# Convolution weights turned after the first k^T v, v loaded by ScalarE's queue, q of batch 1 turned by TensorE

## The chip, the cores and the metric

The kernel runs on one core of a Trainium2 chip. The metric is the device time of one execution in microseconds (us); before the change it is 333.07 us, the median of three runs (332.60 to 333.87). The profile shows one execution, with a span of 331.5 us.

## What is computed

Two blocks follow each other, on 8 batches, 8 heads, 576 tokens and a head width of 64; the 8 heads side by side are the 512 channels of the second block. The inputs q, k and v are float32; the weights of the second block come as float64.

```python
kv   = einsum('bhsd,bhse->bhde', k, v)               # 64 x 64 for each batch and head
out  = einsum('bhsd,bhde->bhse', q, kv)
x    = out / sqrt(mean(out * out, -1) + 1e-6) * g_norm
x    = x.transpose(0, 2, 1, 3).reshape(8, 576, 512)
gate = sigmoid(sum(conv_w[t] * x_shifted_by(4 - t) for t in range(5)))   # causal, by channel
y    = (gate * (x @ w_val)) @ w_out
```

## The kernel before, in words

All work is written as named steps, and the string PLAN at the head of the file lists them, with their arguments, in the order in which they are issued. No scheduler changes it at build time: each engine executes its own instructions in the order of the list, and waits for semaphores where a step needs what another engine makes. The list itself was made by a planner outside the file. So a change of PLAN changes what each engine has queued behind what.

A batch goes through these steps. load_half, load_tails and load_q (or load_q_rows) bring k, v, their last 64 tokens, and q. kv_product (L433) forms k^T v for pairs of heads in the PSUM bank "kv", kv_copy (L453, on ScalarE) moves it into a block-diagonal matrix. q has to lie with its channels across the partitions: turn_q (L463) does this by VectorE's transposes of 32x32 blocks; for batch 0, turn_q_rows (L477) does it by TensorE, five groups of matmuls with the identity into "mm" banks, which sort_q (L487, ScalarE) copies into qT. raw_product (L494) multiplies qT by the matrix, 128 tokens at a time (chunks 0 to 3, and 4 with the last 64 tokens); square (ScalarE), sums (VectorE), powers (GpSimd) and normalise (VectorE for batch 0, ScalarE for the others) make x of it. turn_x and keep_x, or turn_blocks and move_blocks from batch 2 on, put x with its channels across the partitions; halo adds the tokens before. gate_start, four gate_tap and gate_end make the gate; val_product, or from batch 2 on val_fast with fewer multiplications, makes the values; gated multiplies; out_product, or fast_product for the last two batches, is the output projection, and store writes it.

PSUM has eight banks for four kinds (L226): one "kv", two "raw", one "tp", four "mm". The "mm" banks go round among turn_q_rows, val_product, out_product and, for batch 0, raw_product of the chunks 4, 1 and 0.

Before the first batch can be finished, the float64 weights must be made float32. stage_weight loads one piece, narrow_weight turns it in eight small steps 0 to 7: steps 1, 2 and 3 on ScalarE, the others on VectorE. For the convolution weights ("cw", 20 rows) there follow turn_cw (L410), one transpose on TensorE, and keep_cw (L415) on VectorE. They are first used by gate_start.

keep_warm n (L426) issues n matmuls of the identity with itself into the spare half of the "kv" bank. They compute nothing; they fill time in which TensorE would be idle. In the profile every float32 matmul has two records, so keep_warm 5 reads as "x10".

Loads are issued by three queues: SyncE's (SPq) for nearly all, ScalarE's (ACTq) for the first half of k and of v of batch 0 and for the first piece of the value weights, GpSimd's for the convolution weights and g_norm. load_q (L310) brings one pair of heads in four transfers of 32 partitions; load_q_rows (L324) brings four heads in one transfer of 128 partitions, with rows of 18 tokens. Both write into the three slots of the tile qs.

Of the kernel before, what the change touches and what calls it, by code (L numbers as in the profile page):

```python
# [20 lines left out]
stage_weight wval 0; warm_up; load_half k 0 1; load_half v 0 1; stage_weight wval 1; narrow_weight cw 0 0;  # L21
load_half k 1 0; narrow_weight cw 0 1; narrow_weight cw 0 2; load_half v 1 0; narrow_weight cw 0 3;
load_tails 1; narrow_weight cw 0 4; narrow_weight cw 0 5; narrow_weight cw 0 6; narrow_weight cw 0 7;
keep_warm 26; turn_cw; load_half k 1 1; load_half v 1 1; load_q 1 0; keep_warm 5; turn_q_rows 0 0;
turn_q_rows 0 1; sort_q 0 0; turn_q_rows 0 2; sort_q 0 1; kv_product 0 0; narrow_weight wval 0 0; keep_cw;
turn_q_rows 0 3; narrow_weight wval 0 1; sort_q 0 2; turn_q_rows 0 4; narrow_weight wval 0 2; load_q 1 1;
sort_q 0 3; keep_warm 4; kv_product 0 1; sort_q 0 4; load_q 1 2; kv_copy 0; narrow_weight wval 1 0;
narrow_weight wval 0 3; keep_warm 4; raw_product 0 3; narrow_weight wval 1 1; raw_product 0 2; square 0 3;
stage_weight wval 2; stage_weight wval 3; raw_product 0 4; sums 0 3; square 0 2; raw_product 0 1; square 0 4;
powers 0 3; sums 0 2; narrow_weight wval 1 2; narrow_weight wval 0 4; raw_product 0 0; square 0 1; sums 0 4;  # L30
narrow_weight wval 0 5; powers 0 2; square 0 0; normalise 0 3; narrow_weight wval 1 3; sums 0 1; keep_warm 5;
turn_x 0 3; powers 0 4; keep_x 0 3; normalise 0 2; sums 0 0; powers 0 1; keep_warm 5; turn_x 0 2;
normalise 0 4; narrow_weight wval 1 4; keep_x 0 2; narrow_weight wval 0 6; keep_warm 4; turn_x 0 4; powers 0 0;
kv_product 1 0; normalise 0 1; keep_x 0 4; turn_q 1 0; turn_x 0 1; narrow_weight wval 1 5; halo 0; load_q 1 3;
narrow_weight wval 0 7; kv_product 1 1; keep_x 0 1; normalise 0 0; turn_q 1 1; turn_x 0 0; val_product 0 0 1;
narrow_weight wval 1 6; stage_weight wout 0; keep_x 0 0; narrow_weight wval 1 7; gate_start 0 1; turn_q 1 2;
gate_start 0 2; val_product 0 1 1; load_q 2 1; narrow_weight wval 2 0; gate_tap 0 2 3; narrow_weight wval 2 1;
gate_tap 0 1 3; narrow_weight wval 2 2; val_product 0 0 0; gate_tap 0 1 2; gate_start 0 0; load_q 2 0;
gate_tap 0 2 2; narrow_weight wval 2 3; kv_copy 1; narrow_weight wval 3 0; turn_q 1 3; narrow_weight wval 3 1;
load_half k 2 0; narrow_weight wval 2 4; keep_val 0 0 1; keep_warm 6; raw_product 1 3; narrow_weight wval 3 2;  # L40
load_half v 2 0; narrow_weight wval 2 5; load_tails 2; raw_product 1 2; narrow_weight wval 2 6; square 1 3;
keep_val 0 1 1; val_product 0 1 0; sums 1 3; keep_val 0 0 0; narrow_weight wval 3 3; narrow_weight wval 2 7;
load_half v 2 1; powers 1 3; square 1 2; load_half k 2 1; narrow_weight wout 0 0; gate_tap 0 2 1; load_q 2 2;
val_product 0 2 1; sums 1 2; normalise 1 3; narrow_weight wval 3 4; powers 1 2; narrow_weight wval 3 5;
gate_tap 0 2 0; stage_weight wout 2; narrow_weight wout 0 1; keep_warm 3; raw_product 1 1;
narrow_weight wval 3 6; gate_tap 0 0 3; turn_x 1 3; square 1 1; val_product 0 2 0; narrow_weight wout 0 2;
sums 1 1; keep_x 1 3; narrow_weight wval 3 7; powers 1 1; normalise 1 2; gate_tap 0 1 1; val_product 0 3 1;
turn_q 2 0; gate_tap 0 1 0; normalise 1 1; load_q 2 3; raw_product 1 0; turn_q 2 1; turn_x 1 2; val_sums 0;
square 1 0; tail_and_kv 1; narrow_weight wout 0 3; stage_weight wout 1; sums 1 0; keep_x 1 2;
narrow_weight wout 0 4; powers 1 0; keep_val 0 1 0; gate_tap 0 0 2; keep_val 0 2 0; gate_end 0 1; val_sums 1;  # L50
keep_val 0 2 1; turn_x 1 1; turn_q 2 2; square 1 4; normalise 1 0; val_product 0 3 0; sums 1 4; load_q 3 1;
narrow_weight wout 2 0; powers 1 4; narrow_weight wout 0 5; gate_tap 0 0 1; keep_x 1 1; turn_q 2 3; kv_copy 2;
keep_warm 2; turn_x 1 0; load_q 3 0; normalise 1 4; val_sums 2; raw_product 2 3; narrow_weight wout 0 6;
keep_x 1 0; gate_tap 0 0 0; keep_val 0 3 1; turn_x 1 4; square 2 3; raw_product 2 2; narrow_weight wout 0 7;
load_half k 3 1; keep_x 1 4; narrow_weight wout 2 1; sums 2 3; load_half v 3 0; val_product 1 0 1;
gate_end 0 0; load_tails 3; powers 2 3; square 2 2; gated 0 0; narrow_weight wout 2 2; val_product 1 0 0;
gated 0 1; keep_val 0 3 0; load_half v 3 1; narrow_weight wout 2 3; load_half k 3 0; sums 2 2; gate_start 0 3;
stage_weight wout 3; narrow_weight wout 2 4; powers 2 2; normalise 2 3; val_product 1 1 1; load_q 3 2;
gate_tap 0 3 3; narrow_weight wout 1 0; narrow_weight wout 2 5; halo 1; keep_val 1 0 1; gate_tap 0 3 2;
keep_val 1 0 0; raw_product 2 1; normalise 2 2; turn_q 3 0; val_product 1 1 0; turn_q 3 1; load_q 3 3;  # L60
square 2 1; turn_blocks 2 3; narrow_weight wout 1 1; sums 2 1; val_product 1 2 1; keep_val 1 1 1;
gate_tap 0 3 1; narrow_weight wout 1 2; powers 2 1; keep_val 1 1 0; narrow_weight wout 2 6;
narrow_weight wout 1 3; turn_blocks 2 2; raw_product 2 0; gate_end 0 2; narrow_weight wout 1 4; normalise 2 1;
val_product 1 2 0; narrow_weight wout 2 7; narrow_weight wout 1 5; gated 0 2; square 2 0; gate_tap 0 3 0;
tail_and_kv 2; turn_blocks 2 1; gate_end 0 3; narrow_weight wout 3 0; keep_val 1 2 1; sums 2 0;
narrow_weight wout 3 1; narrow_weight wout 1 6; powers 2 0; narrow_weight wout 3 2; gated 0 3;
val_product 1 3 1; load_half k 4 0; narrow_weight wout 3 3; turn_q 3 2; load_half v 4 0; square 2 4; kv_copy 3;
load_half k 4 1; sums 2 4; narrow_weight wout 3 4; normalise 2 0; load_q 4 0; val_product 1 3 0; powers 2 4;
narrow_weight wout 3 5; turn_q 3 3; normalise 2 4; narrow_weight wout 3 6; raw_product 3 3; load_q 4 1;
narrow_weight wout 1 7; gate_start 1 0; turn_x 2 4; narrow_weight wout 3 7; raw_product 3 2; gate_start 1 1;  # L70
turn_blocks 2 0; keep_x 2 4; out_product 0 3; gate_tap 1 0 3; keep_val 1 2 0; move_blocks 2 3; load_tails 4;
keep_val 1 3 1; square 3 3; gate_tap 1 1 3; gate_start 1 2; sums 3 3; square 3 2; load_half v 4 1;
gate_tap 1 0 2; keep_val 1 3 0; powers 3 3; gate_tap 1 2 3; out_product 0 1; sums 3 2; gate_tap 1 1 2;
powers 3 2; normalise 3 3; gate_tap 1 0 1; gate_tap 1 2 2; gate_tap 1 0 0; keep_out 0 3; raw_product 3 1;
move_blocks 2 2; gate_tap 1 1 1; store 0 3; gate_end 1 0; out_product 0 0; gate_tap 1 2 1; square 3 1;
keep_out 0 1; gated 1 0; load_q 4 2; sums 3 1; gate_start 1 3; gate_tap 1 1 0; powers 3 1; gate_tap 1 3 3;
gate_end 1 1; out_product 0 2; turn_blocks 3 3; store 0 1; normalise 3 2; halo 2; gate_tap 1 3 2;
gate_tap 1 2 0; normalise 3 1; move_blocks 2 1; gate_tap 1 3 1; gated 1 1; raw_product 3 0; gate_end 1 2;
gate_tap 1 3 0; tail_and_kv 3; turn_q 4 0; gate_end 1 3; gated 1 2; keep_out 0 0; load_q 4 3; square 3 0;
gated 1 3; sums 3 0; out_product 0 5; weight_sums 0; kv_copy 4; powers 3 0; load_half v 5 1; turn_blocks 3 2;  # L80
square 3 4; store 0 0; sums 3 4; turn_blocks 3 1; powers 3 4; turn_q 4 1; normalise 3 0; move_blocks 2 0;
turn_q 4 2; out_product 0 4; keep_out 0 5; normalise 3 4; store 0 5; turn_q 4 3; keep_out 0 2; weight_sums 1;
turn_blocks 3 0; load_tails 5; turn_x 3 4; val_sums 3; raw_product 4 3; keep_x 3 4; move_blocks 3 3;
raw_product 4 2; square 4 3; load_q 5 0; out_product 0 6; sums 4 3; square 4 2; keep_out 0 4; sums 4 2;
gate_start 2 0; powers 4 3; x_sums 2 0; load_half k 5 0; gate_start 2 3; load_half k 5 1; x_sums 2 1;
gate_start 2 2; gate_tap 2 0 3; val_fast 2 0 0; gate_tap 2 2 3; val_fast 2 0 1; x_sums 2 3; val_keep 2 0 0;
# [100 lines left out]
def kernel(  # L187
# [11 lines left out]
    nc = tc.nc  # L199
# [7 lines left out]
    TB = 32  # L207
# [8 lines left out]
    TURNED_X = 2  # L216
# [608 lines left out]
```

## Time and profile before

| | us |
|---|---|
| time, median of three runs | 333.07 |
| span of the profiled execution | 331.5 |
| TensorE busy (96%) | 319.7 |
| VectorE busy (75%) | 247.0 |
| ScalarE busy (57%) | 189.6 |
| GpSimd busy (43%) | 142.8 |
| keep_warm, 64 matmuls in all | 20.5 |
| turning q of batch 0 on TensorE, 36 matmuls | 6.1 |
| the five copies of it on ScalarE | 2.6 |
| turning q of batch 1 on VectorE, 4 transposes | 3.1 |

The page of a profile gives busy time by engine, then the span in 40 slices with a digit for the busy tenths of each, then the chain of work that ended last. The chain is followed back from the last instruction: at each step to what released it, or to the instruction before it on its engine. A wait for several things is put down to the one that came last. Matmuls are pipelined, so that a busy TensorE isn't always at its peak; the row PEclk and the column of the clock tell at what share of full speed it was allowed to run.

### The profile page before, as it was taken

The numbers are of one execution on the slowest core, as the hardware profiler recorded it, in microseconds if no ns is written. First come the engines' busy times: TensorE is split into PE (matmuls) and PEld (weight loads), VectorE is DVE, ScalarE is ACT, GpSimd is POOL, SyncE is SP. The second block draws the span as 40 slices with busy tenths as digits, with TensorE's granted clock in tenths as the row PEclk, the third lists the DMA queues.
The fourth block names the chain that finished last, engine by engine and source line by source line (L and its number), as shares of the span: only waits on it lengthen the run. The fifth ranks groups of instructions, "written<-read, shape, count | busy, mean of one in ns | idle before, by whom it ended". The sixth has DMA issues, their size and how long they took to land.

```text
span 331.5 us, 6118 instructions
## 1 busy us (share of the span) xinstructions
PE 319.7 (96%) x2041; PEld 230.0 (69%) x2041; DVE 247.0 (75%) x434; ACT 189.6 (57%) x530; POOL 142.8 (43%) x185
## 2 busy tenths in 40 slices
PE   8498999999999999999999999999999999999994
PEld 8498988878854658756884767586544765868652
DVE  1203998999999969998989888978996179835711
ACT  1145487999879664676757655766652344142311
POOL 5002805536469869533985453854749200000000
PEclk9879999999999999999999999999999999999999
DMA  8997289989798778965799884325125203021323
GB/s 275 315 307 216 89 252 308 238 244 289 201 274 237 204 207 232 287 148 147 232 275 261 226 193 128 86 48 127 35 61 156 70 15 75 9 64 32 97 63 95
DMA packets 44127, 56.47 MB, mean 170 GB/s; under 512 B 15158, under 2 KB 33590, under 8 KB 44096
## 3 DMA queue, kind: packets, MB, share of 16 engines
q1 hardware_dynamic: 39120, 47.93, 52.3%
q0 software_dynamic: 3168, 6.32, 7.5%
q10 hardware_dynamic: 1808, 1.84, 1.8%
q8 instruction: 16, 0.26, 0.4%
q14 instruction: 15, 0.12, 0.1%
HBM read 40.33 MB, written 9.44 MB: 150 GB/s over the span
## 4 chain that ended last, share of the span: by engine, by line
PE 90%; POOL 2%; ACT 2%; DMA 2%; DVE 1%; issue 1%; POOLq 0%; ACTq 0%; DVEq 0%
PE out L686 25%; PE va L655 14%; PE raw L501 10%; PE val L605 8%; PE vc L655 7%; PE kv L441 5%; PE out L693 4%; PE a L750 4%; PE vb L655 4%; PE cb L750 3%; PE kv L430 3%; DMA w_cw<-in_moe_conv_w_dram 2%; PE qTps L483 2%; PE xTps L555 1%; POOL rt L529 1%; ACT x L540 1%
## 5 line engine op out<-in xcount | busy, mean ns | idle before, releaser
L529 POOL TENSOR_TENSOR rt<-ss,mhalf 128x8 f32<-128x8 f32 (+1 forms) x40 | 69.6, 1743 | 101.1 <-DVE ss L523 101.0
L593 DVE SCALAR_TENSOR_TENSOR gate<-xT,cwT,gate 128x576 f32<-128x576 f32 x128 | 100.5, 811 | 7.1 <-ACT gate L587 6.6
L686 PE MATMUL out<-wout,gv 128*128 128x512 f32 x192 | 85.6, 594 | 0.0
L686 PEld LDWEIGHTS out<-wout,gv 128*128 128x128 f32 x192 | 35.8, 190 | 39.7 <-issue 37.5
L540 ACT ACTIVATE x<-raw,rt 128x64 f32<-128x64 f32 x252 | 55.3, 345 | 6.9 <-POOL rt L529 6.6
L576 POOL DMA_DIRECT2D xT<-y x96 | 53.3, 561 | 12.0 <-issue 3.4
L523 DVE TENSOR_REDUCE ss<-sq 128x8 f32<-128x520 f32 (+1 forms) x40 | 25.2, 632 | 22.3 <-ACT sq L515 22.1
L501 PEld LDWEIGHTS raw<-kvbd,qT 128*128 128x128 f32 (+1 forms) x320 | 35.1, 180 | 7.9 <-issue 3.7
L501 PE MATMUL raw<-kvbd,qT 128*128 128x128 f32 (+1 forms) x320 | 38.1, 278 | 0.0
L605 PE MATMUL val<-xT,wval 128*128 128x288 f32 x128 | 32.6, 408 | 0.0
L515 ACT ACTIVATE sq<-raw 128x512 f32<-128x512 f32 (+1 forms) x40 | 22.7, 571 | 12.0 <-PE raw L501 11.9
L600 ACT ACTIVATE gate<-gate 128x576 f32<-128x576 f32 x32 | 22.5, 712 | 10.3 <-DVE gate L593 10.3
L701 ACT COPY ot<-out 128x512 f32<-128x512 f32 x28 | 16.4, 591 | 20.4 <-PE out L686 12.4
L605 PEld LDWEIGHTS val<-xT,wval 128*128 128x128 f32 x128 | 23.6, 190 | 6.1 <-DVE wval L387 0.2
L655 PE MATMUL va<-xs,vsum 128*128 128x288 f32 x96 | 27.2, 406 | 0.0
L618 DVE TENSOR_TENSOR gv<-gv,gate 128x576 f32<-128x576 f32 x32 | 23.7, 751 | 2.3 <-ACT gv L676 1.8
L587 ACT ACTIVATE gate<-xT,cwT 128x576 f32<-128x576 f32 x32 | 24.6, 790 | 1.2 <-DVE gv L618 0.8
L430 PE MATMUL kv<-ident 128*128 128x128 f32 x128 | 20.5, 323 | 2.8 <-ACT kvbd L456 1.4
L430 PEld LDWEIGHTS kv<-ident 128*128 128x128 f32 x128 | 19.0, 233 | 4.1 <-ACT kvbd L456 2.4
L655 PEld LDWEIGHTS va<-xs,vsum 128*128 128x128 f32 x96 | 18.1, 190 | 5.2 <-issue 0.5
L469 DVE STREAM_TRANSPOSE qT<-qs 128x512 f32<-128x512 f32 x24 | 16.7, 696 | 0.4 <-DMA qs<-in_q_dram 0.4
L583 POOL COPY xT<-xT 128x124 f32<-128x124 f32 x32 | 16.1, 541 | 1.7 <-DMA xT<-y 1.7
(114 smaller groups left out, 439.3 us busy)
## 6 DMA issues: line engine op xcount, KB each, us to landing
qs<-in_q_dram SPq DMA_DIRECT2D x112, 140.0 KB, 4.2
out_dram<-ot SPq DMA_DIRECT2D x140, 64.0 KB, 1.7
k<-in_k_dram SPq DMA_DIRECT2D x12, 512.0 KB, 5.8
v<-in_v_dram SPq DMA_DIRECT2D x12, 512.0 KB, 5.5
xT<-y POOLq DMA_DIRECT2D x96, 64.0 KB, 3.1
w_wout<-in_moe_w_out_dram SPq DMA_DIRECT2D x4, 512.0 KB, 7.8
y<-in_moe_w_val_dram SPq DMA_DIRECT2D x3, 512.0 KB, 4.6
qs<-in_q_dram SPq DMA_DIRECT2D x2, 576.0 KB, 4.8
```

What stands on the lines that cost most here:

```text
L430: nc.tensor.matmul(st["spare"].rearrange("p h d -> p (h d)")[:, 0:P], ident[:], ident[:], start=True, stop=True)
L501: nc.tensor.matmul(raw[row * m:(row + 1) * m, col * P:(col + 1) * P], st["qT", b][:, hp, c * P:c * P + m], kv_bd[b % 2][:, hp, :], start=T ...
L523: nc.vector.reduce_sum(out=ss[:, 0:n], in_=st["sq", b, c][:, 0:n], axis=AX.X)
L529: nc.gpsimd.tensor_tensor(out=rt[:, 0:n], in0=st["ss", b, c][:, 0:n], in1=mhalf[:, 0:n], op=ALU.pow)
L540: nc.scalar.activation(out=x[:, to * D:(to + 1) * D], in_=st["raw", b, c][:, h * D:(h + 1) * D], func=AF.Copy, scale=st["rt", b, c][:, h:h ...
L576: nc.gpsimd.dma_start(out=xTs[b % 2][i * TB:(i + 1) * TB, :, first:first + P], in_=y[a * TB:(a + 1) * TB, i])
L587: nc.scalar.activation(out=gate[:], in_=xTs[b % 2][:, jt, HALO:SX], func=AF.Copy, scale=cwT[:, K - 1, jt:jt + 1])
L593: nc.vector.scalar_tensor_tensor(out=gate[:], in0=xTs[b % 2][:, jt, tap * TB:tap * TB + S], scalar=cwT[:, tap, jt:jt + 1], in1=gate[:], op ...
L605: nc.tensor.matmul(val[:], wval[:, kc, jt * P:(jt + 1) * P], xTs[b % 2][:, kc, HALO + n * SV:HALO + (n + 1) * SV], start=(kc == 0), stop=( ...
L618: nc.vector.tensor_tensor(out=both, in0=both, in1=st["gate", b, jt][:], op=ALU.mult)
L655: nc.tensor.matmul(st[bank, "val", b, mj][:], weights_[:, k], tokens()[:, k], start=(n in (0, 1, 3) and k == 0), stop=(k == NK // 2 - 1), ...
L686: nc.tensor.matmul(po[:], gv[:, jt, first:first + P], wout[:, jt, :], start=(jt == 0), stop=(jt == NK - 1),)
```

## The change

It has four parts. The narrowing of the convolution weights, turn_cw and keep_cw move in PLAN behind the start of k^T v of batch 0; they stood in front of the turning of q. The second half of v of batch 0 is loaded by ScalarE's queue instead of SyncE's, and the first piece of the value weights by SyncE's instead of ScalarE's. q of batch 1 is loaded by load_q_rows and turned by turn_q_rows and sort_q, as that of batch 0 is, so that turn_q's form for it goes. And the rest of PLAN is planned anew around this: the same steps in another order. The number of fillers goes from 64 to 32. The purpose is that TensorE begins useful work with q as soon as q is there, and that VectorE is relieved of four transposes.

The plan is cut to its beginning, as far as the first product with the value weights; after it only the order changes.

```diff
 load_half k 0 0; stage_weight cw 0; load_q_rows 0 0; load_half v 0 0; load_q_rows 0 1; load_tails 0;
-stage_weight wval 0; warm_up; load_half k 0 1; load_half v 0 1; stage_weight wval 1; narrow_weight cw 0 0;
-load_half k 1 0; narrow_weight cw 0 1; narrow_weight cw 0 2; load_half v 1 0; narrow_weight cw 0 3;
-load_tails 1; narrow_weight cw 0 4; narrow_weight cw 0 5; narrow_weight cw 0 6; narrow_weight cw 0 7;
-keep_warm 26; turn_cw; load_half k 1 1; load_half v 1 1; load_q 1 0; keep_warm 5; turn_q_rows 0 0;
-turn_q_rows 0 1; sort_q 0 0; turn_q_rows 0 2; sort_q 0 1; kv_product 0 0; narrow_weight wval 0 0; keep_cw;
-turn_q_rows 0 3; narrow_weight wval 0 1; sort_q 0 2; turn_q_rows 0 4; narrow_weight wval 0 2; load_q 1 1;
-sort_q 0 3; keep_warm 4; kv_product 0 1; sort_q 0 4; load_q 1 2; kv_copy 0; narrow_weight wval 1 0;
-narrow_weight wval 0 3; keep_warm 4; raw_product 0 3; narrow_weight wval 1 1; raw_product 0 2; square 0 3;
-stage_weight wval 2; stage_weight wval 3; raw_product 0 4; sums 0 3; square 0 2; raw_product 0 1; square 0 4;
-powers 0 3; sums 0 2; narrow_weight wval 1 2; narrow_weight wval 0 4; raw_product 0 0; square 0 1; sums 0 4;
-narrow_weight wval 0 5; powers 0 2; square 0 0; normalise 0 3; narrow_weight wval 1 3; sums 0 1; keep_warm 5;
-turn_x 0 3; powers 0 4; keep_x 0 3; normalise 0 2; sums 0 0; powers 0 1; keep_warm 5; turn_x 0 2;
-normalise 0 4; narrow_weight wval 1 4; keep_x 0 2; narrow_weight wval 0 6; keep_warm 4; turn_x 0 4; powers 0 0;
-kv_product 1 0; normalise 0 1; keep_x 0 4; turn_q 1 0; turn_x 0 1; narrow_weight wval 1 5; halo 0; load_q 1 3;
-narrow_weight wval 0 7; kv_product 1 1; keep_x 0 1; normalise 0 0; turn_q 1 1; turn_x 0 0; val_product 0 0 1;
+load_half v 0 1; warm_up; keep_warm 16; turn_q_rows 0 0; load_half k 0 1; turn_q_rows 0 1; sort_q 0 0;
+turn_q_rows 0 2; stage_weight wval 0; sort_q 0 1; stage_weight wval 1; turn_q_rows 0 3; sort_q 0 2;
+turn_q_rows 0 4; load_q_rows 1 0; keep_warm 1; kv_product 0 0; load_q_rows 1 1; load_half k 1 0;
+narrow_weight cw 0 0; narrow_weight cw 0 1; load_half v 1 0; narrow_weight cw 0 2; load_tails 1;
+narrow_weight cw 0 3; sort_q 0 3; narrow_weight cw 0 4; keep_warm 5; kv_product 0 1; narrow_weight cw 0 5;
+sort_q 0 4; narrow_weight cw 0 6; narrow_weight cw 0 7; turn_cw; kv_copy 0; narrow_weight wval 0 0;
+narrow_weight wval 0 1; load_half k 1 1; keep_warm 3; raw_product 0 3; load_half v 1 1; narrow_weight wval 1 0;
+raw_product 0 2; keep_cw; stage_weight wval 2; square 0 3; stage_weight wval 3; narrow_weight wval 0 2;
+raw_product 0 4; sums 0 3; stage_weight wout 0; square 0 2; raw_product 0 1; powers 0 3;
+narrow_weight wval 1 1; sums 0 2; square 0 4; narrow_weight wval 0 3; keep_warm 2; turn_q_rows 1 0; square 0 1;
+powers 0 2; normalise 0 3; narrow_weight wval 1 2; sums 0 4; sort_q 1 0; keep_warm 2; turn_x 0 3; sums 0 1;
+turn_q_rows 1 1; powers 0 4; keep_x 0 3; normalise 0 2; narrow_weight wval 1 3; powers 0 1; turn_x 0 2;
+normalise 0 4; narrow_weight wval 0 4; turn_q_rows 1 2; keep_x 0 2; narrow_weight wval 1 4; turn_x 0 4;
+normalise 0 1; keep_x 0 4; narrow_weight wval 1 5; sort_q 1 1; keep_warm 3; raw_product 0 0; halo 0;
+narrow_weight wval 1 6; turn_x 0 1; narrow_weight wval 1 7; square 0 0; turn_q_rows 1 3;
+narrow_weight wval 0 5; sort_q 1 2; sums 0 0; keep_x 0 1; turn_q_rows 1 4; narrow_weight wval 0 6; powers 0 0;
+sort_q 1 3; kv_product 1 0; load_q 2 0; narrow_weight wval 0 7; sort_q 1 4; narrow_weight wval 2 0;
+kv_product 1 1; narrow_weight wval 2 1; normalise 0 0; narrow_weight wval 2 2; narrow_weight wval 3 0;
+val_product 0 0 1;
...
@@ load_half
-                (nc.sync if i else nc.scalar).dma_start(
+                (nc.sync if i and name == "k" else nc.scalar).dma_start(
@@ stage
-        (nc.gpsimd if key[0] == "cw" else nc.scalar if key == ("wval", 0) else nc.sync).dma_start(
+        (nc.gpsimd if key[0] == "cw" else nc.sync).dma_start(
@@ turn_q
-        if b < TURNED_X:
-            nc.vector.transpose(out=qT, in_=q[:, :, 0:TB])
-            return
```

## The prediction

> **What bounds the kernel now.** I read the page first: of a span of 331.5 us TensorE is busy for 319.7.
>
> ```profile
> PE 319.7 (96%) x2041; PEld 230.0 (69%) x2041; DVE 247.0 (75%) x434; ACT 189.6 (57%) x530; POOL 142.8 (43%) x185
> PE   8498999999999999999999999999999999999994
> PEclk9879999999999999999999999999999999999999
> ```
>
> So the end is set by when TensorE gets useful work and by how little filler and waiting lies in it. Only the first slices of 8.3 us show a hole, and there the granted clock falls too. Next I read the chain that ended last, in order of time (start, us, what):
>
> ```profile
> 5.30 6.69 DMA w_cw<-in_moe_conv_w_dram
> 14.96 2.43 PE kv L430 x10
> 17.39 4.59 PE qTps L483 x48
> ...
> 25.54 1.36 PE kv L441 x40
> 27.73 1.16 PE kv L430 x8
> 28.88 4.36 PE raw L501 x40
> 33.25 1.12 PE kv L430 x10
> 34.80 1.12 PE kv L430 x10
> 36.35 0.89 PE kv L430 x8
> 37.48 1.31 PE kv L441 x40
> ```
>
> The chain begins with the transfer of the convolution weights. TensorE's queue is in order, and turn_cw (L410) stands in front of turning q; it waits until the weights have landed at 12.0 and been narrowed until 14.6. The ten records of L430 are five fillers. Useful work starts at 17.39 and the first raw_product only at 28.88. Last, busy time by stretch (columns: stretch, its us, then PE, PEld, DVE, ACT, POOL busy, clock, DMA share, GB/s):
>
> ```profile
> 11.00:12.00 1.00, 0.00 (x0) 0.00 (x0) 0.00 (x0) 0.00 (x0) 0.00 (x0) 1.00 1.10 258
> 17.00:18.00 1.00, 1.00 (x8) 0.78 (x9) 0.26 (x1) 0.00 (x0) 0.00 (x0) 0.50 1.06 347
> ...
> 60.00:70.00 10.00, 9.46 (x134) 8.40 (x133) 9.19 (x19) 9.59 (x33) 3.17 (x2) 1.00 0.86 230
> 70.00:80.00 10.00, 10.00 (x52) 8.19 (x51) 9.47 (x18) 10.00 (x31) 5.49 (x7) 1.00 1.04 279
> ```
>
> TensorE stands idle from 10.3 to 14.7, and afterwards runs at half clock until 21.0. From 31 to 110 VectorE is busy for more than 9 of every 10 us, and ScalarE comes close between 60 and 80; after that only TensorE is full.
>
> **What the Trainium skill says.** "TensorE: Matmul & The Clock Gate", Part 1: the clock halves after an idle window of about 3.4 us and doubles after as long a busy one. The trace agrees: a gap of 4.4 us is followed by a clock of 0.50 for 6.6 us. The table at the head of that page has ScalarE and VectorE take their queues strictly in order, so a copy of q waits behind whatever stands before it on ScalarE; the trace has nothing against it. "DMA: Bandwidth & Descriptors", Issuing engines are not separate DMA queues: issuing from another engine saves only issue time. The trace agrees in that 12 to 19 us moves 330 to 350 GB/s whatever queue the loads come from.
>
> **The change part by part.**
>
> *Convolution weights behind k^T v.* The first useful matmul then waits for q alone. q's two transfers are issued at 0.74 and 1.17 and land 3.8 and 5.8 us later, so at 4.5 and 7.0. Sixteen fillers (two records each, six records per us at half clock) run from 1.36 to about 6.8, so turning q starts at 7.0 with no gap and soon at full clock. It is 72 records; 24 of them took 1.31 at full clock (chain at 23.14), so 3.9: done at 11.0. turn_cw costs one transpose of 0.3 behind work; narrowing it takes 12.0 to 14.6 on VectorE and ScalarE, which have nothing else. The two last copies of q stand behind it on ScalarE and are through by 14.5; nothing needs them before raw_product.
>
> *Both halves of v on ScalarE's queue.* k^T v of batch 0 needs k, v and the 64-token tails. In the compiled order each transfer waits for the landing of the one eight places before it. By the landings of before, the last tail can be issued at 8.6 (behind v's first part) and lands about 5.5 later, at 14.1; the second half of k is issued at 9.7 and lands 4.6 later, at 14.3; the second half of v is issued by 5.1 and is long there. So TensorE turns q until 11.0, does 16 records of k^T v, waits for tails until 14.1 (an idle time of 2.5, below the 4.4 that cost the clock), then the rest of the first half 0.8, five fillers 1.1, the second half 1.2: 17.2. kv_copy took 0.74 and its start 0.2; three fillers 0.7: raw_product at 18.7, against 28.88. That is 10.2 earlier. The weights of the value projection, moved to the sync queue, land about 15 to 16; they are first narrowed after 16.
>
> *q of batch 1 by TensorE.* Added: 72 records, 3.9 us of TensorE, and five copies, 2.6 us of ScalarE (group L490, 542 ns each). Removed: four transposes, 3.1 us of VectorE (group L467). Also 16 transfers of 140 KB become two of 576 KB; before, the 12 issues from 18.70 took 11.3 us and held the next weights back until 30.07. That relief costs nothing and hides behind other work. Removed as well are fillers: the chain has 50 records after the first raw_product, 6.0 us; 14 remain, 1.6 us. On TensorE this nearly cancels: +3.9 -4.4 = -0.5.
>
> *The new wait.* The first raw_products are followed by square 0.60, sums 0.69, powers on GpSimd, normalise 0.69. Five powers took 8.00 in a row, about 1.7 for a full one and 1.1 for the short one. In the new order the fourth ends at 19.6 + 0.6 + 0.7 + 0.2 + 6.3 = 27.4. raw_product 0 0 has moved behind it: it takes a "mm" bank that normalise 0 1 frees at 28.2. Queued behind it on TensorE are turn_x 0 1, two groups of turns and k^T v of batch 1: 28.2 + 0.9 + 0.4 + 1.3 = 30.8 for the latter, against 37.48. All of batch 1's k and v, the eighth MB, is there at about 27 (8.1 MB at 310 to 340 GB/s), so this wait is not the transfer's. From here before had 2.9 of fillers left (12, 6 and 4 records) and the new order none, and 0.4 of turn_x is already done: 37.5 - 30.8 + 2.9 + 0.4 = 10.0 earlier.
>
> *The dense stretch.* Behind it TensorE has the same work, but loses its slack: ScalarE has to do 2.6 more by then, and its 9.6 to 10 of 10 from 60 to 80 leaves no room; VectorE's 3.1 less helps by as much where it is the one that is late. Bounds: nothing, if ScalarE makes it up between 40 and 60 (7.5 and 7.9 of 10), or 2.6 in full. I take 1.0. The replanned order of the rest moves no work between engines; the stalls there are some 2 us in 235, so it can give little and lose a little; I take 0.6 lost. VectorE's and ScalarE's other moved instructions cost nothing beyond this, since TensorE's matmuls lie over them.
>
> Sum: 10.0 - 1.0 - 0.6 = 8.4; 333.07 - 8.4 = 324.7 us.
>
> **The rivals.**
>
> *The dense stretch eats half of it.* VectorE is at 9.2 to 10 of 10 from 31 to 110 and ScalarE will now be as full; if neither can go ahead of TensorE any more, waits of both kinds add up to 4 or 5 us. For it: the three engines have nearly the same sum of work there. Against it: VectorE's work falls by 3.1 and begins 10 us earlier too. 333.07 - 10.0 + 4.5 + 1 = 328.6.
>
> *The clock falls again.* If the wait for tails is nearer 3.5 than 2.5, the clock halves at about 14 for as long as before, and 0.8 + 1.1 + 1.2 of matmuls and fillers and part of the raw_products double: 3 to 4 lost. For it: transfers of 64 KB took 4.8 to 7.2 to land. Against: 16 records of k^T v lie in the gap. 324.7 + 3.3 = 328.
>
> *Everything fits.* The dense stretch costs nothing and the new order of the rest is a little better: 333.07 - 10.0 - 1.5 = 321.6.
>
> *Slower.* Loads of batches 1 and 2 are needed 7 to 10 us earlier. The share of the DMA engines is already 0.8 to 1.1 from 40 to 130; if batch 2's seven loads, which may begin only when q of batch 1 has been turned at about 31, miss k^T v of batch 2 (some 20 us later, for 3.5 MB, or 12.5 at 280 GB/s), TensorE waits, the clock may halve, and later batches inherit it. To end above 334.7 that takes 10 us of new stalls: 335.5. Against it: 8 us of margin, and from batch 2 on the buffers are freed at the same distance from their use as before.
>
> **How the numbers follow.** Forecast (323 to 326.5) 0.50, dense stretch 0.20, clock 0.10, everything fits 0.13, slower 0.04, something in between that ends within 0.5% 0.03. The likeliest gives 324.7. The range takes the forecast, the two middle cases and most of the good one: 320.8 to 329.8. Faster 0.93, same 0.03, slower 0.04.
>
> **What would show it.** In the chain of waits, the convolution weights and the cold turns at 17.39 are gone; turn_q_rows starts near 7; raw_product near 18.7; k^T v of batch 1 near 31. The clock stays at 1.00 after 8 us. In the stretches, ScalarE is above 9 in 10 for some 40 us. The prediction is wrong if the first raw_product starts after 21 (tails or k late), if k^T v of batch 1 starts after 34 (powers or transfers), or if TensorE idles by more than 3 us in all between 31 and 120.

## The result and the profile after

The changed kernel takes 323.69 us (median of four runs, 323.16 to 324.43) against 332.84 for the kernel before, run beside it: a ratio of 0.9728, with a 95% interval of 0.9689 to 0.9767. The prediction was 324.7 with a range of 320.8 to 329.8. The gain is 9.15 us where 8.4 were forecast.

From the page of the changed kernel, as from the page of before: the busy times of the engines, TensorE by slices and the granted clock.

```profile
PE 313.4 (97%) x2049; PEld 223.2 (69%) x2049; DVE 246.2 (76%) x430; ACT 191.8 (59%) x535; POOL 146.3 (45%) x185
PE   8899999899999999999999999999999999999994
PEclk9999999999999999999999999999999999999999
```

The hole in the second slice has gone and the clock never falls. TensorE is busy for 6.3 us less although it now turns q of batch 1 as well: part of the work before was done at half clock, and 32 fillers are gone.

The chain that ended last, in order of time (start, us, what), for the stretch up to k^T v of batch 1:

```profile
1.75 6.76 DMA v<-in_v_dram
8.53 5.25 DMA vl<-in_v_dram
...
13.92 0.88 PE kv L443 x22
14.80 1.31 PE kv L432 x10
16.11 1.34 PE kv L443 x40
...
18.27 0.94 PE kv L432 x6
19.20 3.47 PE raw L500 x32
...
28.23 0.67 PE kv L432 x6
28.90 0.89 PE raw L500 x8
...
30.23 1.46 PE qTps L482 x24
31.69 2.33 PE kv L443 x80
```

The chain no longer begins with the convolution weights. It begins with the first part of v, behind whose landing the last tail (part of the last 64 tokens of v) is issued, at 8.53; that tail lands at 13.78. raw_product starts at 19.2 instead of 28.88, and k^T v of batch 1 at 31.69 instead of 37.48. From there to the end it takes 290.9 instead of 294.0 us: 5.8 + 3.1 make the 8.9 by which the two profiled spans differ (331.5 and 322.6).

Busy time by stretch (its us, then PE, PEld, DVE, ACT, POOL busy, clock, DMA share, GB/s), first where TensorE waits for the tails, then in the dense part:

```profile
12.00:13.00 1.00, 0.39 (x11) 0.25 (x6) 0.43 (x3) 0.97 (x4) 0.00 (x0) 1.00 1.02 314
13.00:14.00 1.00, 0.08 (x3) 0.11 (x5) 0.54 (x2) 0.23 (x1) 0.00 (x0) 1.00 1.08 341
...
60.00:70.00 10.00, 9.27 (x49) 7.69 (x49) 9.95 (x18) 9.68 (x27) 4.43 (x2) 1.00 1.10 311
70.00:80.00 10.00, 10.00 (x123) 8.34 (x122) 10.00 (x20) 9.83 (x33) 5.79 (x7) 1.00 0.62 161
```

TensorE idles from 12.4 to 13.9 with its clock at 1.00, and in the dense part it is busy for 9.3 and 10 of 10 us while VectorE and ScalarE are both at 9.7 to 10. All waits of TensorE up to 110 us (what for: us in total, times, longest), apart from the one at the very start:

```profile
PE kv L443 <- DMA vl<-in_v_dram: 1.5, 1, 1.5
...
PE xTps L554 <- ACT xT L561: 0.7, 1, 0.7
PE kv L432 <- ACT kvbd L458: 0.7, 1, 0.7
PE xTps L554 <- ACT x L539: 0.4, 1, 0.4
```

The wait of 4.4 for the convolution weights has become one of 1.5 for a tail. ScalarE's added copies show up in no more than 1.1 us of waits of turn_x (0.7 and 0.4).

### The profile page after: what moved, and what is told of

It reads as the page before. It is cut to its first block, busy times and chain, and to the rows that moved or that the text cites. A ratio compares the mean times of both kernels' runs of the same rounds, so it can differ in the third digit from the quotient of the medians.

```text
span 322.6 us, 6073 instructions
## 1 busy us (share of the span) xinstructions
PE 313.4 (97%) x2049; PEld 223.2 (69%) x2049; DVE 246.2 (76%) x430; ACT 191.8 (59%) x535; POOL 146.3 (45%) x185
## 4 chain that ended last, share of the span: by engine, by line
PE 89%; DMA 4%; ACT 3%; POOL 2%; DVE 1%; ACTq 0%; issue 0%; POOLq 0%
PE out L685 26%; PE va L654 15%; PE raw L500 10%; PE val L604 7%; PE vc L654 7%; PE kv L443 5%; PE out L692 4%; PE a L749 4%; PE vb L654 4%; PE cb L749 3%; DMA v<-in_v_dram 2%; POOL rt L528 2%; DMA vl<-in_v_dram 2%; PE qTps L482 1%; ACT x L539 1%; PE xTps L554 1%
## 5 line engine op out<-in xcount | busy, mean ns | idle before, releaser
L528 POOL TENSOR_TENSOR rt<-ss,mhalf 128x8 f32<-128x8 f32 (+1 forms) x40 | 74.0, 1856 | 85.2 <-DVE ss L522 85.1
L539 ACT ACTIVATE x<-raw,rt 128x64 f32<-128x64 f32 x252 | 55.5, 338 | 17.7 <-POOL rt L528 17.5
L567 DVE STREAM_TRANSPOSE y<-x 128x512 f32<-128x512 f32 x24 | 16.7, 701 | 2.1 <-ACT x L539 2.0
L443 PE MATMUL kv<-v,k 128*64 128x64 f32 x448 | 17.1, 222 | 0.0
L443 PEld LDWEIGHTS kv<-v,k 128*64 128x64 f32 x448 | 16.0, 138 | 0.2
```

Source lines behind the costliest of these rows:

```text
L443: nc.tensor.matmul(kvp[r * D:(r + 1) * D, hp, :], kl[:, head(hp, r), :] if j == NJ else st["k", b, at[0]][:, at[1], at[2], j, :], vl[:, he ...
L528: nc.gpsimd.tensor_tensor(out=rt[:, 0:n], in0=st["ss", b, c][:, 0:n], in1=mhalf[:, 0:n], op=ALU.pow)
L539: nc.scalar.activation(out=x[:, to * D:(to + 1) * D], in_=st["raw", b, c][:, h * D:(h + 1) * D], func=AF.Copy, scale=st["rt", b, c][:, h:h ...
```

## The experiments

Theory 1 was: what is gained before the first raw_product comes out at the end one for one, and most of it comes from the convolution weights. The rivals were those of the prediction (the dense stretch, the clock, late transfers), and that part C, q of batch 1 by TensorE, earns much of the gain. Unless said otherwise each kernel is the changed one with one edit, and its median is set against before in runs on the same chip (332.84 beside the changed kernel, later 332.36, 332.24 and 332.16). These medians of before differ by up to 0.7 us between chips, so a difference of less than 1 us between two kernels from different chips says little. Each kernel has one profile, of one of its executions; what is read from it holds for that execution. In the texts put down before each run, rival 2 is that the other parts carry the gain, rival 3 that VectorE's relief does, theory 4 that fewer bytes of q do, and rival 5 that fewer transfers do.

### Undo A: convolution weights in front again (e1_cw_first)

```diff
+narrow_weight cw 0 0; ... narrow_weight cw 0 7; keep_warm 26; turn_cw; keep_warm 5;
-keep_warm 16;
 turn_q_rows 0 0; ...
-narrow_weight cw 0 0..7; turn_cw    (around kv_product 0 0 and 0 1)
+keep_cw;                            (ahead of kv_product 0 0)
-keep_cw;                            (behind raw_product 0 2)
```

> The changed kernel, but with the convolution weights narrowed and turned ahead of the turning of q again, and 26 and 5 fillers around that as before; all else as changed. Theory 1 (the time at which TensorE begins useful work passes to the end one for one): turning starts at about 17 with a halved clock, the first raw_product near 28, the end 9 us later than the changed kernel, 332 to 333.5. Rival 2 (the other parts and the new order of the rest carry most of it): below 327.

Measured: 333.52 us, ratio 1.0032 (1.0017 to 1.0046): the whole gain is gone, and a little more. From the chain in order of time:

```profile
15.80 4.94 PE qTps L482 x72
...
26.88 3.47 PE raw L500 x32
...
39.36 2.33 PE kv L443 x80
```

Against the changed kernel's profile the first raw_product is 7.7 us later (26.88 for 19.20), k^T v of batch 1 7.7 later (39.36 for 31.69), and the end 7.7 later (330.3 for 322.6). In this pair of executions one for one holds exactly, over 300 us. (They are the fastest of this kernel's and the slowest of the changed one's; the medians are 9.8 apart.) But the run also shows that without A the other parts, as planned here, give nothing: 1.2 us slower than before.

### A alone on the kernel before (e4_before_cw_behind)

```diff
 (before.) -narrow_weight cw 0 0..7; keep_warm 26; turn_cw; keep_warm 5; turn_q_rows 0 0;
+keep_warm 16; turn_q_rows 0 0; ... kv_product 0 0; narrow_weight cw 0 0..3; ...
+turn_q_rows 0 4; narrow_weight cw 0 4..7; ... kv_product 0 1; turn_cw; ... raw_product 0 3; keep_cw;
```

> The kernel before with one edit: the convolution weights are narrowed and turned behind k^T v of batch 0, with 16 fillers in front of q instead of 26 and 5. Order of the rest, loads and q of batch 1 as before. Theory 1: turning at 7, first raw_product near 19.2, and the end 9 us or so earlier than the kernel before: 323.5 to 326. Rival 2 (the other parts are needed for it): above 328.5, since the loads and VectorE's order were planned for a later start.

Measured: 325.96 us, ratio 0.9806 (0.9762 to 0.9850): 6.4 of the 9.15 us. The chain:

```profile
7.28 2.77 PE qTps L483 x48
...
19.28 4.36 PE raw L501 x40
...
27.87 1.32 PE kv L441 x40
...
33.15 7.08 DMA qs<-in_q_dram
```

The queue of transfers, for the last pair of q of batch 1:

```profile
30.95 2.63 SPq L317 DMA_DIRECT2D qs<-in_q_dram  x4
```

The start is as early as in the changed kernel: raw_product at 19.28, which is 9.6 before 28.88, and k^T v of batch 1 at 27.87 even 3.8 earlier than in the changed kernel. Yet the end comes only 7.7 earlier than in the profile of before. The chain then runs into the last pair of q of batch 1, which lands at 40.2; its raw_product follows at 40.7, against 36.6 in the changed kernel. So with the early start the transfers of q of batch 1 become the limit, and the other parts are worth something only then: -6.4 for A alone, +1.2 for the rest alone, -9.15 together. The slots bear on this too: the tile qs has three for the four pairs, so the last pair goes into that of the first and can be loaded only after the first transpose (29.14 to 29.92), while two row loads need no slot twice. Whether that holds it back here isn't shown, since SyncE issues the transfers ahead of it until 30.85. The two figures for one part alone come from plans made for something else: e4 keeps the order of before and 49 fillers where the changed kernel has 32, and no run takes the new order of the rest by itself.

### Undo B: the second half of v by SyncE's queue (e2_v_by_sync)

```diff
-load_half v 0 1; warm_up; ... load_half k 0 1; turn_q_rows 0 1; ... turn_q_rows 0 2; stage_weight wval 0;
+stage_weight wval 0; warm_up; ... load_half k 0 1; load_half v 0 1; turn_q_rows 0 1; ... turn_q_rows 0 2;
-                (nc.sync if i and name == "k" else nc.scalar).dma_start(
+                (nc.sync if i else nc.scalar).dma_start(
-        (nc.gpsimd if key[0] == "cw" else nc.sync).dma_start(
+        (nc.gpsimd if key[0] == "cw" else nc.scalar if key == ("wval", 0) else nc.sync).dma_start(
```

> The changed kernel, but with the second half of v of batch 0 on the sync queue again, behind that of k, and the first piece of the value weights on the scalar queue. v then lands at about 15.4 as in the kernel before; the second half of k^T v started at 16.0 in the changed kernel, behind five fillers. Theory 1: 0 to 0.5 us later than the changed kernel, 323.5 to 324.3. Rival (the queue of v pays): 1 us or more later, above 324.7.

Measured: 325.40 us (324.32 to 328.72), ratio 0.9804 (0.9736 to 0.9873). TensorE's instructions in the profiled execution (start, us, engine, line, operation, out<-in, form, count, in brackets the idle time before and what ended it):

```profile
16.65 0.30 PE L443 MATMUL kv<-v,k 128*64 128x64 f32 x2 [1.66 <-DMA v<-in_v_dram]
17.37 0.59 PE L443 MATMUL kv<-v,k 128*64 128x64 f32 x13 [0.42 <-DMA v<-in_v_dram]
...
21.09 5.60 PE L500 MATMUL raw<-kvbd,qT 128*128 128x128 f32 x32
```

The second half of v is now the last to land, at 16.5 and 17.2 (10.5 and 11.8 in the changed kernel, where it doesn't stand behind k and the tails in SyncE's queue). TensorE idles for 1.7 and 0.4 us shortly after each other, and then the clock halves: it reads 0.62 from 18 to 20 us and 0.50 up to 24, and the 32 records of raw_product take 5.60 instead of 3.63 us. Of four executions two kept a clock of 0.997 or more and took 324.3 and 324.5, 0.7 us more than the changed kernel; the others had 0.995 and 0.988 and took 326.3 and 328.7. So the median lies where the rival has it, but because of the clock, which fell in two of four executions here and in none of the changed kernel's four. What v's queue is worth without the clock, 0.7 us in two executions on another chip, is not shown.

### No fillers around the second half (e5_no_fillers_kv), and not those at the start (e6_no_start_fillers)

```diff
-keep_warm 5; kv_product 0 1;      e5
+kv_product 0 1;
-keep_warm 3; raw_product 0 3;
+raw_product 0 3;

-keep_warm 16; turn_q_rows 0 0;    e6
+turn_q_rows 0 0;
```

> The changed kernel without the five fillers ahead of the second half of k^T v of batch 0 and without the three ahead of the first raw_product. The second half of k landed at 15.1, and the fillers hold TensorE until 16.0; the three take 0.7. Theory 1: the first raw_product comes 1.5 us earlier and the end with it, 322.0 to 322.8, as long as the clock stays at full. Rival (the clock): with the gaps at 12.4 to 13.9, about 14.7 to 15.2 and 16.6 to 17.4 the clock halves in some executions, and the time is 1 to 4 us above the changed kernel in these.

> The changed kernel without the sixteen fillers at the start, so that q is turned from 7 at half clock. 72 records at 97 ns take 7 us if the clock stays at half, so until 14.0, when the tails have just landed; the clock rises after some 4 to 6 us of work. Theory 1: the turns have 2.7 us of room ahead of the tails, 0 to 1 us later than the changed kernel, 323.7 to 324.8. Rival (the clock counts more): 3 us later or more, above 326.5.

e5: 324.56 us, ratio 0.9764 (0.9724 to 0.9803), and six executions that differ: 322.3 and 322.9 with a clock of 0.998 and 0.999, 324.0 to 326.6 with 0.988 to 0.992. So without the eight fillers the time is 0.8 to 1.4 us below the changed kernel's median where the clock holds, and 0.3 to 2.9 above it where it doesn't. TensorE in the profiled execution, which is one of the latter:

```profile
15.01 0.24 PE L443 MATMUL kv<-vl,kl 128*64 128x64 f32 x1 [2.29 <-DMA vl<-in_v_dram]
...
16.34 0.90 PE L443 MATMUL kv<-v,k 128*64 128x64 f32 x13 [0.41 <-DMA k<-in_k_dram]
...
19.46 5.49 PE L500 MATMUL raw<-kvbd,qT 128*128 128x128 f32 x32 [0.61 <-ACT kvbd L458]
```

Idle times of 2.3 and 0.4 us with work between them are enough: the clock reads 0.61 from 16 to 18 us, ahead of the third idle time of 0.6. The 2.3 is the wait for the tails, which landed at 14.9 in this execution and at 13.8 in the profile of the changed kernel, and which the edit doesn't touch. That the missing fillers matter rests on counting executions: the clock fell in four of six here, and in none of the twelve of the three kernels with the same loads and the five fillers (the changed one, e6 and f2: 0.997 or more). The Trainium skill, "TensorE: Matmul & The Clock Gate", Part 1, tells of an idle window of some 3.4 us; the 4.4 us of the kernel before agree, but here no single idle time is near it. The changed kernel, with gaps of 1.5 and 0.7 us and fillers between, kept 0.998 or more in all four executions.

e6: 324.48 us, ratio 0.9763 (0.9736 to 0.9790), which can't be told from the changed kernel's 0.9728.

```profile
6.84 6.19 PE L482 MATMUL qTps<-ident,qs 128*64 128x128 f32 x70 [1.55 <-DMA qs<-in_q_dram]
...
19.00 1.17 PE L500 MATMUL raw<-kvbd,qT 128*128 128x128 f32 x9
```

Turning q starts cold (6.19 us for 70 records, 4.15 for 72 in the changed kernel) and ends at 13.0 instead of 11.2. That raw_product still starts at 19.0 is luck in this execution: its last tail landed at 12.0, so TensorE never waited for it, and the first half of k^T v followed the turns at 13.4. The changed kernel's chain has 2.6 us of room between the turns and a tail at 13.8, but with a tail at 12.0 it is the turns that bound. So e6 doesn't test that room. Without the start fillers turning ends 1.8 us later, which costs nothing where the tails land late.

### Undo C: q of batch 1 by VectorE (e3_q1_by_vector, e9_q1_vector_kv_first)

```diff
 def turn_q
+        if b < TURNED_X:
+            nc.vector.transpose(out=qT, in_=q[:, :, 0:TB])
+            return
-load_q_rows 1 0; ... load_q_rows 1 1;   +load_q 1 0; load_q 1 1; ... load_q 1 2; ... load_q 1 3
-turn_q_rows 1 0..4; sort_q 1 0..4;      +turn_q 1 0..3 at the places of sort_q 1 0, 1, 2 and 4
 e9: load_q 1 0..2 behind load_half v 1 1
```

> The changed kernel, but with q of batch 1 loaded pair by pair and turned by VectorE again, its four transposes where the copies stood. TensorE has 3.9 us less, ScalarE 2.6 less, VectorE 3.1 more. Theory 1: the turns lay in the waits for powers, so most of TensorE's 3.9 doesn't come back, and VectorE has room: 322.5 to 325. Rival 3 (VectorE bounds the stretch up to 110, and its relief pays): 326.5 or more.

> As the run with q of batch 1 turned by VectorE, but with twelve of its sixteen transfers behind k and v of batch 1 instead of ahead of them. Theory 4: TensorE no longer waits for v of batch 1 from 29.4 to 32.4, and what is left is the wait for the last pair of q, which stands behind a transpose and the weights: 325 to 329. Rival 3 (VectorE's four transposes cost by themselves): 331 or more, as in that run.

Measured: e3 335.17 us, ratio 1.0074 (1.0054 to 1.0094); e9 334.94, ratio 1.0083 (1.0046 to 1.0121). Both are 11 us slower than the changed kernel, and both expectations of 322 to 329 failed; the numbers lie where the rival had them. But the four transposes take only 3.1 us of VectorE, so it isn't their time. In e3, waits of TensorE up to 60 us, and below them VectorE's last transpose, from its timeline:

```profile
PE xTps L556 <- ACT wexp_wval L367: 3.7, 1, 3.7
PE kv L442 <- DMA wsum<-in_v_dram: 2.7, 1, 2.7
PE xTps L556 <- DVE x L545: 2.1, 2, 1.6
```

```profile
40.27 0.78 DVE L468 STREAM_TRANSPOSE qT<-qs 128x576 f32<-128x576 f32 x1 [7.18 <-DMA qs<-in_q_dram]
```

The longest wait is put down to ScalarE, but ScalarE itself waits for VectorE, which stands for 7.2 us at the transpose of the last pair until its transfers have landed. The second: q's twelve small transfers stand ahead of k and v, and k^T v of batch 1 waits for v. e9 takes that second wait away by loading k and v first. Then its waits begin with the first line here; below it VectorE's first transpose, from its own timeline:

```profile
PE xTps L556 <- DVE x L545: 6.8, 2, 6.3
```

```profile
28.52 0.78 DVE L468 STREAM_TRANSPOSE qT<-qs 128x576 f32<-128x576 f32 x1 [4.61 <-DMA qs<-in_q_dram]
```

VectorE stands for 4.6 us with nothing to do, because the transpose at the head of its queue waits for q; the sums and the normalise behind it, which batch 0 needs, wait with it, and TensorE waits 6.3 for the result. Behind such waits the clock falls as well, in e9 to 0.50 from 26 to 36 us; its mean was 0.972 to 0.988 in the twenty executions of e3. So these two kernels show what a plan made for one form costs when the other form is put into its slots; they don't show what VectorE's form would cost in a plan of its own. e4 is nearer to that, and is 2.3 us slower than the changed kernel, with the reservations made there.

### Bytes or number: q of batch 1 read twice, or in 16 parts (e8_q1_read_twice, e8b_q1_bytes_only, e10_q1_rows_in_16)

e3 and e4 point to the transfers of q. load_q reads every head of it twice: 16 transfers, 2.24 MB; load_q_rows 1.15 MB in two. These runs take the two differences apart.

```diff
 def load_q_rows, b == 1:
         nc.sync.dma_start(out=qs[:, r]..., in_=q[b, r * (H // 2):(r + 1) * (H // 2)]...)
+        nc.sync.dma_start(out=qs[:, 2]..., in_=the same)               e8
+        nc.sync.dma_start(out=gv[:, 2 + r, 0:NB * D], in_=the same)    e8b
-        (the one transfer)                                             e10
+        for a in range(H // 2), half in range(2): nc.sync.dma_start(
+            out=qs[a * TB:(a + 1) * TB, r, half of n], in_=q[b, r * (H // 2) + a, half of n])
```

> The changed kernel, with q of batch 1 loaded a second time into the third slot, which nobody reads: two transfers of 576 KB more, 2.3 MB in all, the bytes that loading pair by pair has. Nothing else changes on any engine. In the changed kernel the last part of v of batch 1 lands at about 29.7 and is needed at 31.5. Theory 4 (the bytes of q in the full stretch of the transfers are what the part on q saves): 1.15 MB at 330 GB/s is 3.5 us, so v lands at 33 and the end comes 1.5 to 3 us later, 325.2 to 327. Rival 5 (the number of transfers and their places among the eight in flight count, not their bytes): 0 to 0.5 us later.

> The changed kernel with each of the two row loads of q of batch 1 followed by a second load of the same 0.59 MB into a part of the gated-values tile that nobody reads before it is written anew (1.15 MB more bytes, two more transfers, no transfer waiting for another one's destination; the outputs stay what they were). Theory 'bytes' (the share of the transfers in the gain of part C is that of the moved bytes: load_q moves 2.24 MB where the rows move 1.15 MB): at the 340 to 410 GB/s of the first 20 us the extra bytes take 2.8 to 3.4 us, the last part of v of batch 1 lands at 32.5 to 33.1 instead of 29.7, the first k^T v of batch 1 that needs it, at 31.5, waits 1 to 1.6, time 324.6 to 325.6. Rival 'number' (what holds back is the count of the transfers and not their size): two more transfers of some 30 already issued, time 323.5 to 324.2.

> The changed kernel with the two row loads of q of batch 1 cut into 16 (one for each head and half of the row; 32 partitions each; the same bytes). Theory 'number': as with the 16 transfers of load_q, every one of them takes a place among the few under way and holds back the loads of k and v behind it: the second row load ends later by several us, v of batch 1 lands at 33 or later instead of 29.7, time 326 to 331. Rival 'bytes': the queue only has to issue 14 more, 323.5 to 324.5.

e8: 326.40 us, ratio 0.9804 (0.9770 to 0.9839). It doesn't answer the question, since both extra loads have one destination: in the queue of transfers the second is issued 6 us late, when the first has landed, and everything behind it waits.

```profile
13.77 0.69 SPq L328 DMA_DIRECT2D qs<-in_q_dram  x1
20.72 0.33 SPq L332 DMA_DIRECT2D qs<-in_q_dram  x1
```

e8b, with two destinations, has no such wait: 325.71 us (324.66 to 327.75), ratio 0.9815 (0.9764 to 0.9866), 2 us more than the changed kernel. The wait it adds:

```profile
PE kv L447 <- DMA wsum<-in_v_dram: 0.8, 1, 0.8
```

v of batch 1 lands at 32.0, and k^T v of batch 1, which could have gone on at 31.3, goes on at 32.1. In the changed kernel the same part of v, issued at 21.4, lands 7.2 us later, at 28.5 (not at 29.7, as the expectations have it). So in this execution the 1.15 MB cost 3.4 us of landing, of which 0.8 reached TensorE, and the profiled time is 1.0 above the changed kernel's; the rest of the 2 us between the medians is not explained by this profile. Bytes count once the room is used up: the changed kernel needs v 3 us after it lands.

e10, with the same bytes: 327.84 us, ratio 0.9865 (0.9839 to 0.9891), 4 us more than the changed kernel. The queue of transfers, then TensorE:

```profile
12.44 10.91 SPq L332 DMA_DIRECT2D qs<-in_q_dram  x16
```

```profile
24.76 1.74 PE L490 MATMUL qTps<-ident,qs 128*64 128x128 f32 x14 [1.81 <-DMA qs<-in_q_dram]
26.43 1.22 PE L440 MATMUL kv<-ident 128*128 128x128 f32 x4
```

Sixteen transfers of 72 KB take 10.91 us to be issued, where two of 576 KB took 1.62: the expectation for "number" holds. (One issue takes SyncE 0.42 us in the median of the sixteen, and 0.41 for a transfer of 576 KB.) What it hits is not v, as I had expected, but q itself: TensorE waits 1.8 for it at 22.9, the clock halves at 25 (four fillers take 1.22 instead of 0.61), and the rest comes 3.3 us later (k^T v of batch 1 at 34.80, and at 31.52 in the same timeline of the changed kernel). So in the changed kernel's plan the part of C that pays is above all that q of batch 1 comes in two large transfers to all partitions (number, width and the length of the pieces are not told apart here), and in second place that it comes once. What the slots contribute, which load_q runs out of, no run separates.

### Two versions meant to be faster (f2_no_three_fillers, f1_tails_last)

```diff
-keep_warm 3; raw_product 0 3;                                          f2
+raw_product 0 3;

-keep_warm 5; kv_product 0 1; ... turn_cw; kv_copy 0; ... keep_warm 3; raw_product 0 3;   f1
+keep_warm 11; kv_product 0 1; kv_tails 0; ... kv_copy 0; ... raw_product 0 3; turn_cw;
 def kv_product: the tails (j == NJ) of batch 0 left to kv_tails, which takes all eight
```

> The changed kernel without the three fillers ahead of raw_product (the five ahead of the second half of k^T v stay). They stood behind the copy of k^T v (18.27 to 19.2), since they write into the bank that the copy reads. Theory 1: raw_product starts at 18.3 instead of 19.2 and the end comes 0.9 earlier: 322.7 to 323.0. Rival 'clock': TensorE idles from 17.6 to 18.3, after 1.5 ahead of the tails and with little else, and its clock falls in some executions, as without both sets of fillers, where four of six lost 1 to 3 us: median 324 to 325, with a wide spread.

> A version meant to be faster: in the first k^T v of batch 0 the eight products over the tails come last, behind both halves, so that the first half does not wait for the tails (13.9); eleven fillers instead of five ahead of the second half bridge the wait for its k (15.1); the three fillers ahead of raw_product, which waited for the copy of k^T v, are gone, and the convolution weights are turned behind raw_product. Theory 1 (one for one): k^T v ends at about 16.6 instead of 17.4, raw_product starts at 17.5 instead of 19.2, end 1.6 earlier: 322.1, if v of batch 1 (29.7) does not come too late for a k^T v of batch 1 at 29.9. Rival 'transfers': v of batch 1 is needed at 29.9 and lands no earlier, half of the gain is lost: 322.8 to 323.5. Rival 'clock': the wait of about 0.9 for the copy halves TensorE's clock in some executions: 324 to 326.

f2: 322.89 us (322.28 to 323.22), ratio 0.9715 (0.9688 to 0.9742), with a clock of 0.997 to 1.000 in all four executions. It is the fastest run of this study, but its interval lies over that of the changed kernel (0.9689 to 0.9767), so 0.8 us is not shown as a difference. Its chain:

```profile
13.51 1.31 PE kv L432 x10
14.82 1.36 PE kv L443 x40
...
17.00 3.73 PE raw L500 x32
```

From the end of k^T v to raw_product it is 0.8 us, where the changed kernel needs 1.75: the three fillers stood behind the copy out of their bank. That step is as expected. That raw_product starts at 17.0 has a second cause: in this execution the last tail had landed at 12.5, before TensorE asked for it, so it didn't wait, and the span is 320.5. One for one holds again: raw_product is 2.2 us earlier than in the changed kernel's profile, the end 2.1.

f1: 323.90 us (323.66 to 324.63), ratio 0.9751 (0.9724 to 0.9778), missing the 322.1 expected. The chain:

```profile
12.64 2.65 PE kv L432 x22
15.29 1.08 PE kv L443 x32
...
17.68 1.16 PE raw L508 x8
...
30.79 2.33 PE kv L443 x80
```

raw_product starts at 17.68, near the expected 17.5, but with no wait at all on the way: the eleven fillers end at 15.29 and the second half begins at once, so they, and not a transfer, set the time. f2 has shown that the second half can begin at 14.82. Of the 1.5 us gained at raw_product 0.9 are left at k^T v of batch 1 (30.79 for 31.69), in part because turn_cw now stands between the raw_products, and 0.7 at the end of the profiled execution (321.9 for 322.6); the medians don't differ beyond what two chips do. Of k^T v of batch 0 this form keeps only the tails for six of the eight heads, which leaves its number of instructions as it should be. The Trainium skill, "PSUM — Partial Sum Buffer", The four PSUM rules, says why: a matmul that starts a sum clears the marks of the whole bank, on the partitions it writes, and a later one without a start then overwrites. The run agrees: the relative error of its output is 0.36877, which is what comes out for the tails alone in all heads of batch 0 but 3 and 7, the two whose sums were started last in the bank; with heads 0 and 4 kept in their place it would be 0.3707. A form that may put the tails last must start the bank once.

## Why the prediction was right

**The start.** Turning q begins at 7.05 (7.0 predicted) and ends at 11.2 (11.0); the last tail lands at 13.8 (14.1); k^T v ends at 17.4 (17.2) and raw_product starts at 19.2 (18.7; the terms given for it add up to 18.8). In this profile the tails bound the stretch and not q, as predicted: TensorE waits 1.5 us for them. The weights' narrowing shows up in no wait of TensorE.

**From raw_product to k^T v of batch 1.** Predicted to start at 30.8, it starts at 31.69; so 5.8 us are gained by then and not 6.7. Half of that is the later raw_product. The order of the work in it is as said: raw_product 0 0 behind normalise, then turns, then k^T v.

**From there to the end.** I had 2.9 of fillers and 0.4 of turn_x as gain, and took off 1.0 for the dense stretch and 0.6 for the new order: 1.7 in sum. Measured are 3.1. So the two costs together were 0.2, not 1.6: this is the term that was mis-sized. Busy time from the start of k^T v of batch 1 to the end, before and after:

```profile
37.48:331.50 294.02, 288.76 (x1732) 200.47 (x1732) 236.85 (x396) 175.93 (x505) 131.80 (x164) 1.00 0.59 159
31.69:322.60 290.91, 285.25 (x1706) 197.39 (x1702) 233.06 (x388) 175.88 (x505) 133.01 (x160) 1.00 0.59 157
```

TensorE has 3.5 us less to do there and idles for 5.7 us instead of 5.3: the fillers and the turn_x are gone as forecast, and all the waiting that the dense stretch and the new order add is 0.4. That the whole sum came out so near is in part luck, since the 0.9 too much before this point and the 1.4 too little behind it have opposite signs. ScalarE's 2.6 us of copies lie between 24.3 and 32.2, ahead of that stretch, and from 60 to 80 both engines are as full as feared with only 1.1 us of waits of TensorE on ScalarE. The sign named for this, ScalarE above 9 in 10 for some 40 us, came true for three of the four stretches of 10 us from 40 to 80; from 50 to 60 it has 8.3.

**The step that was wrong** is "That relief costs nothing and hides behind other work", on the transfers of q of batch 1, along with v of batch 1 "there at about 27". v lands at 28.5 and is needed at 31.5, so there the claim that it holds nothing up is right, with little to spare. With q in 16 transfers TensorE waits for q (e10, +4 us), with q's bytes doubled it waits for v (e8b, +2), and with A alone it waits for the last pair of q (e4, 2.3 us slower than the changed kernel). I had priced C as a trade of TensorE's time against fillers, -0.5; that trade is right as far as it goes, but C pays, in these plans, because the early start needs its transfers. The end stayed right since the changed kernel has C.

**Readings that don't hold.** From 12 to 19 us of the kernel before every transfer under way came from SyncE's queue, since ScalarE's last had landed at 11.8; the 330 to 350 GB/s there can't show that the queue doesn't matter. Both queues are at work from 4 to 6 us, with 385 to 405. And the clock took 6.8 us of work to double again (from 14.3 to 21.1), twice the time that the prediction gives for it.

**The rivals.** The dense stretch is not borne out. The clock rival is real and nearer than its chance said: the changed kernel, with 1.5 us of idle time, fillers and v on ScalarE's queue, stays clear of it; without the fillers it came in four of six executions, with v on SyncE's queue in two of four, and in e10 after a single wait of 1.8. The slower rival, loads of batch 2, did not show: no wait for a transfer appears between 31 and 110.

**What stays open.** How much VectorE's 3.1 us would cost in a plan of their own was not measured; e3 and e9 mix it with the order of its queue. What the new order of the rest and the 32 fillers less are worth by themselves was not measured either, nor, of q's transfers, number, width and slots one by one. Whether f2 is truly faster than the changed kernel would need more executions. Why the last tail lands anywhere from 12.0 (e6) to 14.9 (e5) in kernels that load it alike I can't say; this spread is as large as most of the differences looked for here.

## What to carry to other kernels

A wait at the head of an in-order queue near the start is worth its full length at the end if the rest is full; ask what it hides, and move everything out of the way of the first useful work. But an earlier start also brings every later load nearer to its due time, so look at the number and size of the transfers that are needed next before calling them hidden. A gain that depends on two edits can't be read by undoing one: here A alone gave 6.4, the rest alone cost 1.2, and both gave 9.15. And where a transfer lands differently by 2 us from one execution to the next, one profile can't tell which of two steps bounds: look at when it landed before saying so.

## What the runs showed of the hardware that I had not expected

- The clock halved after idle times of 2.3 and 0.4 us with work between them (e5; it fell in four of six executions), and after a single one of 1.8 (e10), though none is near the 4.4 us that halved it before. A wait of 1.9 in e4 and one of 1.5 in the changed kernel left it at full, so the length of the wait alone doesn't decide.
- Summed from the clock columns, it stayed at half for 3.4 us (e1, e10), 6.8 (before, e2, e5) or 10.2 (e9): each time a multiple of 3.4.
- Sixteen transfers of 72 KB to 32 partitions each held the issuing queue for 10.91 us (waits for earlier landings among them), two of 576 KB to 128 partitions for 1.62, with the same bytes.
- A start of one sum in a bank made the next products of other sums in that bank overwrite instead of add (f1, relative error 0.36877).
